# A second batch of attention in float32 products, and subtractions moved from GpSimd to VectorE

## The chip, the cores and the metric

The kernel runs on one core of one Trainium2 chip. The metric is device time in microseconds (us), the median of several runs of one execution each. A core has TensorE (matrix products, written PE, its weight loads PEld), VectorE (DVE), ScalarE (ACT), GpSimd (POOL) and SyncE (SP, here the queue that issues all transfers).

## The reference, cut to what matters

Eight batches of 576 tokens with 512 features go through three blocks, all in float32:

```
q, k, v: (8, 8, 576, 64); attention inside chunks of 64 tokens
  scores = q k^T / 8;  p = softmax(scores);  x = p v          -> (8, 576, 512)
token and channel mixer, for each batch
  u  = x + (relu(x^T w_tok1) w_tok2)^T       w_tok1 576x256, w_tok2 256x576
  x2 = u + relu(u w_ch1) w_ch2               w_ch1 512x1536, w_ch2 1536x512
gated mixer
  h  = relu(x2 w_in);  u, v = the halves of h (512 each)
  v  = (v - mean) / sqrt(var + 1e-6)
  v  = w_spatial v + b_spatial               along the 576 tokens
  out = (u * v) w_out
```

## The kernel before, in words

A float32 factor is split into a half-precision high part and a half-precision low part (`hi = f16(x)`, `lo = f16(x - hi)`), and a product is three half-precision products (hi hi, hi lo, lo hi) that add up in PSUM. The high part is made by ScalarE, the low part by a subtraction on VectorE or GpSimd.

**Weights.** The weights come as 64-bit floats. 24 chunks (list `W`) of up to 1024 columns: 0 and 1 are w_tok1, 2 and 3 w_tok2, 4 to 9 w_ch1, 10 to 15 w_ch2, 16 to 19 w_in, 20 and 21 w_out, 22 and 23 w_spatial (float32, 1440 columns). `w_steps` (lines 115 to 157) gives a chunk's four steps: `upper` (L127, L129) and `lower` (L133) build the float32 from the two words on VectorE, `high` (L140 scales in place, L141 makes the high part; L143 alone for the first six chunks) is ScalarE's, `low` (L148) is GpSimd's, except for the first six chunks, whose subtraction is done by TensorE (L153, L154) and brought back by ScalarE. Loads go to three stage buffers in turn (six for the first six chunks), the float32 to two temporaries in turn. `w_tick` moves the list on by one step, with two chunks under way; `w_until(i)` ticks until chunk i is done.

**Attention.** A group is 128 tokens of a batch (five groups, the last of 64). Batch 0 (`first_steps`, lines 406 to 473) uses float32 products on 64x64 quarters of TensorE: 32 score products a group, maximum and subtraction on VectorE out of PSUM (L426, L427), the exponential on ScalarE, the normalisation on VectorE (L436 to L439), four transposes on TensorE (L444), copied back by ScalarE, and 64 products with v, which give the output both ways round (L455, L457), with the low part by VectorE (L470). Batches 1 to 7 (`at_steps`, lines 230 to 394) have 20 steps a group: load, split q and k (`qk_hi`, `qk_lo`), score products in half precision, softmax (L303 to L314), split p (L317 and, on GpSimd, L320), transpose p by a transfer (L321), split v (L327, L331), products with p, split the output (L383 and, on GpSimd, L386) and transpose it by a transfer (L387). Batch 1 (`ACC`) adds up its three products in PSUM; batches 2 to 7 put the parts side by side in one product (`stack`, `cross_s`, `add_s`, `cross_x`, `add_x`).

**Order.** From line 735 on TensorE's order is as written; the other engines' orders are planned when the program is built, with the written order as priority. Products run through `products`, which calls `pump` after each one: a clock of TensorE's time at full speed, which starts attention steps of the next batch (`attention_from`, spread over 80 us for batch 1 and 118 us after) and weight ticks (one in 1.7 us during batch 0's channel products, one in 3 us from the gate on). PSUM has four tiles of two banks, shared by all.

A batch is: `tok1` (L534, L538), `tok2` (with a residual, L548 to L550), `ch1` (12 blocks of 24 products, L511), `ch2` (4 blocks of 72 products), `gate_v` (statistics L628 to L638, on GpSimd the power L636 and the low part L645), the next batch's `tok1`, then `gated` (`gate_u` and `spatial`), the next `tok2` and the output product L689. In batch 0, `ch1(m)` waits in the written order for chunk 4 + m // 2 and `ch2` for chunk 15; `ch1` of batch 0 is evicted twice by ScalarE (L586, L587) with its low part on GpSimd (L588), in the other batches by L590 and, on VectorE, L591. The residual of `ch2` has its low part on GpSimd for blocks 0 to 2 and on VectorE for block 3 (L557).

Of the kernel before, what the change touches and what calls it, by code (L numbers as in the profile page):

```python
# [15 lines left out]
ACC = 1  # L16
# [10 lines left out]
def mixer_kernel(ctx: ExitStack, tc, qk0, qk, v, wt1, wt2, wc1, wc2, win, wsp, bsp, wout, out):  # L27
# [87 lines left out]
    def w_steps(i):  # L115
# [92 lines left out]
    def at_load_qk(g):  # L208
        b, i, n = geo(g)
        own, cross, cs = ranges(n)  # L210
        if b == ACC:
            SP.dma_start(
                out=qk32.rearrange("p h c t -> p (h c t)")[:, 0:8 * n],
                in_=qk0[b, :, i * 1024:i * 1024 + 8 * n],
            )
            return
# [13 lines left out]
    def at_steps(g):  # L230
# [4 lines left out]
        m = {"acc": b == ACC}  # L235
        xT = xTs[b % 2]

        flat = qt.rearrange("p h s t -> p (h s t)")
        parts = [flat[:, e * 1024:e * 1024 + 8 * n] for e in range(2)]
        raw = qk32.rearrange("p h c t -> p (h c t)")[:, 0:8 * n]  # L240

        def qk_hi():
            if m["acc"]:
                ACT.activation(out=parts[0], in_=raw, func=AF.Copy)
                return
            ACT.activation(out=qt[:, :, own], in_=qk32[:, :, cs], func=AF.Copy)
# [8 lines left out]
        def stack():  # L255
            if m["acc"]:
                return
# [5 lines left out]
        def score():  # L263
            m["sp"] = sp = pm.tile([128, 2, 512], F32, tag="m", name="mp").rearrange(
                "p a (h c t) -> p (a h) c t", h=4, c=2)
            if m["acc"]:
                m["sc"] = sp[:, :, 0, :]
                hi, lo = [p.rearrange("p (s h t) -> p s h t", s=2, h=4) for p in parts]
                for c in range(nc_):
                    t = slice(c * 64, c * 64 + 64)  # L270
                    for h in range(H):
                        r, hh = (LOW, HIGH)[h // 4], h % 4
                        for e, (x, y) in enumerate(((hi, hi), (hi, lo), (lo, hi))):
                            PE.matmul(out=sp[64 * c:64 * c + 64, h, 0, :], lhsT=x[r, 0, hh, t], rhs=y[r, 1, hh, t],
                                      start=(e == 0), stop=(e == 2))
                return
# [5 lines left out]
        def cross_s():  # L282
            if m["acc"]:
                return
# [5 lines left out]
        def add_s():  # L290
            if m["acc"]:
                return
            sd = m["sc"] = m["sd"]
# [4 lines left out]
        def shift():  # L298
            if m["acc"]:
                m["sd"] = sdp.tile([128, H, 64], F32, name="sd")  # L300
            sd, sc = m["sd"], m["sc"]
            m["mx"] = mx = sm.tile([128, H, 1], F32, name="mx")
            DVE.tensor_reduce(out=mx[rows], in_=sc[rows], axis=AX.X, op=ALU.max)  # L303
            DVE.tensor_tensor(out=sd[rows], in0=sc[rows], in1=mx[rows].to_broadcast([n, H, 64]), op=ALU.subtract)  # L304
# [29 lines left out]
        def attend():  # L334
            m["av"] = av = pm.tile([128, 2, 512], F32, tag="m", name="mp").rearrange(
                "p a (k e t) -> p (a k) e t", k=2, e=2)
            if m["acc"]:
                for h in range(H):
                    e = h % 2
                    for c in range(nc_):  # L340
                        q = slice(c * 64, c * 64 + 64)
                        for f in range(2):
                            PE.matmul(out=av[64 * e:64 * e + 64, h // 2, 0, q], lhsT=v16[:, c, h // 2, 2 * e + f, :],
# [507 lines left out]
```

## Time and profile before

| | us |
|---|---|
| median of 3 runs (lowest, highest) | 1207.16 (1206.79, 1207.28) |
| the profiled execution, its own time | 1207.75 |
| its span, first to last instruction | 1206.0 |

| engine | busy us | share of the span | instructions |
|---|---|---|---|
| TensorE products | 1139.4 | 94% | 9472 |
| TensorE weight loads | 820.1 | 68% | 9472 |
| VectorE | 746.8 | 62% | 1256 |
| ScalarE | 458.2 | 38% | 698 |
| GpSimd | 286.9 | 24% | 229 |

The profile is one execution. Times in it are from the span's start. A row of the timeline gives start, duration, engine, line, operation, what it writes and reads, and in brackets the engine's idle time before it and what ended that. "PEclk" and "granted clock" are the share of TensorE's full clock that it had. Batch 0's `tok1` starts at 46.05 us, its first gate product at 179.8 us, and the `tok2` of batch 1 at 244.4 us.

### The profile page before, as it was taken

How to read it: one execution, taken by the hardware profiler on the slowest of the kernel's cores; microseconds unless marked ns; L12 is line 12 of the kernel's file. 1: busy time of each engine (PE TensorE's matmuls, PEld its weight loads, DVE VectorE, ACT ScalarE, POOL GpSimd, SP SyncE). 2: the span in 40 equal slices, each digit the busy share in tenths (PEclk: the TensorE clock that was granted, in tenths of full speed). 3: DMA queues.
4: the chain of work that ended last, by engine and by line, in shares of the span. 5: the costliest groups of instructions: out<-in, count | busy, mean ns of one | idle time of the engine just before them, and what ended most of it. 6: DMA issues, size and time to landing. Idle time of an engine off the chain costs nothing. (4 is left out here: it accounts for less than half of the span.)

```text
span 1206.0 us, 22087 instructions
## 1 busy us (share of the span) xinstructions
PE 1139.4 (94%) x9472; PEld 820.1 (68%) x9472; DVE 746.8 (62%) x1256; ACT 458.2 (38%) x698; POOL 286.9 (24%) x229
## 2 busy tenths in 40 slices
PE   6786887799999999999999999999999999999998
PEld 5464663578757786678857786678858786677765
DVE  6899978865667655865557654775567532542141
ACT  4556444444244433344334433443333422221021
POOL 0167734311122112310222111320232011300120
PEclk9898889799999999999999999999999999999999
DMA  9646444232312412132212422232212211000001
GB/s 334 198 150 187 121 123 129 44 71 66 75 29 60 97 49 67 44 71 50 75 35 57 105 55 66 45 71 45 66 49 45 62 27 36 1 1 1 10 27 44
DMA packets 97138, 87.08 MB, mean 72 GB/s; under 512 B 75664, under 2 KB 76816, under 8 KB 94736
## 3 DMA queue, kind: packets, MB, share of 16 engines
q1 hardware_dynamic: 97040, 85.68, 26.6%
q8 instruction: 74, 1.21, 0.4%
q14 instruction: 24, 0.20, 0.1%
HBM read 59.70 MB, written 9.44 MB: 57 GB/s over the span
## 5 line engine op out<-in xcount | busy, mean ns | idle before, releaser
L511 PE MATMUL mp<-hb,c2w 128*128 128x288 f16 x2304 | 292.7, 289 | 5.4 <-DVE sd L304 3.7
L511 PE MATMUL mp<-xb,c1w 128*128 128x288 f16 x2304 | 289.8, 287 | 5.5 <-DVE sd L304 1.7
L511 PEld LDWEIGHTS <-c1w 128*128 128x128 f16 x2304 | 224.9, 98 | 65.1 <-issue 6.6
L511 PEld LDWEIGHTS <-c2w 128*128 128x128 f16 x2304 | 225.4, 99 | 64.2 <-DVE sd L304 4.0
L591 DVE SCALAR_TENSOR_TENSOR hb<-mp,hb 128x576 f16<-128x576 f32 x84 | 63.2, 753 | 103.5 <-ACT hb L590 103.3
L511 PE MATMUL mp<-spw,vn 128*128 128x288 f16 x896 | 118.8, 290 | 6.5 <-DVE vt L625 4.1
L386 POOL TENSOR_TENSOR xh<-xT,xh 128x512 f16<-128x512 f32 x28 | 38.1, 1362 | 295.5 <-ACT xh L383 251.0
L511 PEld LDWEIGHTS <-vn 128*128 128x128 f16 x896 | 87.6, 99 | 30.3 <-issue 4.3
L511 PE MATMUL mp<-xb,inw 128*128 128x288 f16 x768 | 99.3, 286 | 0.0
L689 PE MATMUL mp<-otw,gb 128*128 128x512 f16 x432 | 96.0, 379 | 0.0
L590 ACT ACTIVATE hb<-mp 128x576 f16<-128x576 f32 x84 | 54.3, 646 | 104.2 <-PE mp L511 104.0
L511 PE MATMUL mp<-inw,xb 128*128 128x512 f16 x384 | 86.0, 384 | 4.8 <-ACT xb L556 4.7
L511 PEld LDWEIGHTS <-inw 128*128 128x128 f16 x768 | 75.1, 98 | 20.5
L320 POOL TENSOR_TENSOR p<-sd,p 128x512 f16<-128x512 f32 (+1 forms) x35 | 42.3, 1210 | 138.7 <-ACT p L317 129.1
L689 PEld LDWEIGHTS <-gb 128*128 128x128 f16 x432 | 42.1, 98 | 47.9
L331 DVE SCALAR_TENSOR_TENSOR v<-v,v 128x512 f16<-128x512 f32 (+1 forms) x70 | 47.5, 705 | 42.8 <-ACT v L327 42.4
L511 PEld LDWEIGHTS <-xb 128*128 128x128 f16 x384 | 37.7, 99 | 51.6 <-ACT xb L556 5.2
L557 POOL TENSOR_TENSOR xb<-rt,xb 128x576 f16<-128x576 f32 x24 | 34.0, 1418 | 159.6 <-ACT xb L556 159.6
L555 DVE SCALAR_TENSOR_TENSOR rt<-mp,xT 128x576 f32<-128x576 f32 x32 | 24.2, 757 | 69.3 <-PE mp L511 68.8
L327 ACT ACTIVATE v<-v 128x1024 f16<-128x1024 f32 (+1 forms) x35 | 33.9, 969 | 62.4 <-PE mp L350 62.4
L511 PE MATMUL mp<-t2w,hb 128*128 128x288 f16 x384 | 52.8, 292 | 3.7 <-ACT hb L540 3.0
L628 DVE BATCH_NORM_STATS2 st<-vt 128x6 f32<-128x512 f32 (+1 forms) x40 | 27.6, 691 | 45.2 <-ACT vt L622 44.9
(152 smaller groups left out, 1475.6 us busy)
## 6 DMA issues: line engine op xcount, KB each, us to landing
qk<-in_qk SPq DMA_DIRECT2D x28, 512.0 KB, 3.8
v<-in_v SPq DMA_DIRECT2D x56, 256.0 KB, 3.8
out<-o SPq DMA_DIRECT2D x31, 256.0 KB, 2.0
vn<-in_wc SPq DMA_DIRECT2D x4, 1024.0 KB, 5.9
otw<-in_wc SPq DMA_DIRECT2D x3, 1024.0 KB, 5.2
spw<-in_wc SPq DMA_DIRECT2D x3, 1024.0 KB, 4.7
hb<-in_qk SPq DMA_DIRECT2D x4, 512.0 KB, 8.0
otw<-in_win SPq DMA_DIRECT2D x2, 1024.0 KB, 6.0
```

What stands on the lines that cost most here:

```text
L320: POOL.tensor_tensor(out=p16[rows, :, 1], in0=m["sd"][rows], in1=p16[rows, :, 0], op=ALU.subtract)
L327: ACT.activation(out=hi_lo[:, :, OWN], in_=v_in, func=AF.Copy, scale=SX)
L331: DVE.scalar_tensor_tensor(out=hi_lo[:, :, 1 + e], in0=v_in[:, :, e], scalar=SX, in1=hi_lo[:, :, 3 * e], op0=ALU.mult, op1=ALU.subtract)
L386: POOL.tensor_tensor(out=m["lo"], in0=xT[:, :, tk], in1=m["hi"], op=ALU.subtract)
L511: PE.matmul(out=o, lhsT=l, rhs=r, start=(i == 0), stop=(i == len(seq) - 1))
L555: DVE.scalar_tensor_tensor(out=t, in0=ps, scalar=DN10, in1=two(x[:, m]), op0=ALU.mult, op1=ALU.add)
L557: eng.tensor_tensor(out=xl, in0=t, in1=xh, op=ALU.subtract)
L590: ACT.activation(out=hh, in_=ps, func=AF.Relu)
L591: DVE.scalar_tensor_tensor(out=hlo, in0=ps, scalar=0.0, in1=hh, op0=ALU.max, op1=ALU.subtract)
L628: DVE.bn_stats(out=st[0:n], in_=t[0:n])
L689: PE.matmul(out=ps, lhsT=gb[:, l, k, tk], rhs=otw[:, r, k], start=(k == 0 and e == 0), stop=(k == 3 and e == 2))
```

## The change

Three things are done. Batch 1 takes the float32 attention of batch 0 (`first_steps` becomes `wide_steps`, with the buffers of the later batches for q, k and v), so the branches for it in `at_steps` go. The low part of every weight chunk from 6 on is one VectorE instruction (`s * scale - hi`), so ScalarE's scaling in place goes, and batch 0's `ch1` is evicted as in the other batches; batch 0's `ch2` has all its low parts on VectorE. And batch 0's `ch2` runs two blocks at a time with k outside, each two k waiting in the written order for their own chunk, from chunk 10. In the beginning, the five q, k loads (and those of v) all go ahead of the first weight load, and weight ticks start at tick 9, not 6.

```diff
         def high():
-            if i >= BY_PE:
-                ACT.activation(out=s, in_=s, func=AF.Copy, scale=scale)
-                ACT.activation(out=hi, in_=s, func=AF.Copy)
-            else:
-                ACT.activation(out=hi, in_=s, func=AF.Copy, scale=scale)
+            ACT.activation(out=hi, in_=s, func=AF.Copy, scale=scale)
...
             if i >= BY_PE:
-                POOL.tensor_tensor(out=lo, in0=s, in1=hi, op=ALU.subtract)
+                DVE.scalar_tensor_tensor(out=lo, in0=s, scalar=scale, in1=hi, op0=ALU.mult, op1=ALU.subtract)
                 return
...
+    def wide_qk(g):
+        b, i, n = geo(g)
+        to = first_qk[:, i * 1024:i * 1024 + 8 * n] if b == 0 else one_qk[:, 0:8 * n]
+        SP.dma_start(out=to, in_=qk0[b, :, i * 1024:i * 1024 + 8 * n])
+
+    def wide_v(b, c0, to):
+        c1 = c0 + to.shape[1]
+        for r, half in enumerate((LOW, HIGH)):
+            SP.dma_start(out=to[half].rearrange("p c h d -> p c (h d)"),
+                         in_=v[b, 64 * c0:64 * c1, r * 256:r * 256 + 256].rearrange("(c k) f -> k c f", k=64))
...
+        steps = [[f] for f in (score, shift, expo, norm, turn, turned, attend, out_hi, out_lo)]
+        if b == 0:
+            return steps
+        steps = [[lambda: wide_qk(g)], [], [], []] + steps
+        steps[5].append(lambda: wide_v(b, 2 * i, vals))
+        return steps + [[]] * (NA - len(steps))
...
-            live[g] = at_steps(g)
+            live[g] = wide_steps(g) if g < 2 * NT else at_steps(g)
...
-    def ch1(m, relax=False):
+    def ch1(m):
...
-        if relax:
-            t = wrk.tile([128, 2, 288], F32, tag="t", name="ht")
-            ACT.activation(out=t, in_=ps, func=AF.Relu)
-            ACT.activation(out=hh, in_=t, func=AF.Copy)
-            POOL.tensor_tensor(out=hlo, in0=t, in1=hh, op=ALU.subtract)
-            return
...
+    def ch2(ms, x):
+        pss = [psum2() for _ in ms]
+        for k in range(12):
+            for i, m in enumerate(ms):
+                mc = slice(m * 128, m * 128 + 128)
+                for e, (a, r) in enumerate(((0, 0), (0, 1), (1, 0))):
+                    for o, s in zip(pss[i][0], HALF):
+                        PE.matmul(out=o, lhsT=c2w[:, a, k, mc], rhs=hb[:, k, r, s], start=(k + e == 0), stop=(k == 11 and e == 2))
+                        pump(288)
+            if len(ms) > 1 and k % 2 and k < 11:
+                w_until(11 + k // 2)
+        for i, m in enumerate(ms):
+            residual(pss[i][1], m, x, DVE if m == 3 or len(ms) > 1 else POOL)
+            DVE.tensor_copy(out=xt[:, m], in_=xb[:, :, m, 512:576])
...
-        first_load(0)
-        first_load(1)
...
+        wide_qk(0)
+        wide_qk(1)
+        wide_v(0, 0, first_v)
         for i in range(2, 5):
-            first_load(i)
+            wide_qk(i)
+        for _ in range(6):
             w_next()
...
-        if tick >= 6:
+        if tick >= 9:
             w_tick()
...
-                ch1(m, b == 0)
-            if b == 0:
-                w_until(15)
-            for m in range(4):
-                ch2(m, x)
+                ch1(m)
+            for ms in ((0, 1), (2, 3)) if b == 0 else ((0,), (1,), (2,), (3,)):
+                if b == 0:
+                    w_until(10)
+                ch2(ms, x)
```

## Rows read from the trace of the kernel before

**Rows 1.** The page: engine shares, and GB/s in 40 slices of the span.

```profile
PE 1139.4 (94%) x9472; PEld 820.1 (68%) x9472; DVE 746.8 (62%) x1256; ACT 458.2 (38%) x698; POOL 286.9 (24%) x229
...
GB/s 334 198 150 187 121 123 129 44 71 66 75 29 60 97 49 67 44 71 50 75 35 57 105 55 66 45 71 45 66 49 45 62 27 36 1 1 1 10 27 44
```

**Rows 2.** Windows: us; busy (count) of PE, PEld, DVE, ACT, POOL; PEclk; DMA share, GB/s.

```profile
64.60:129.40 64.80, 45.68 (x498) 34.69 (x496) 64.66 (x57) 36.86 (x51) 43.52 (x20) 0.91 0.53 160
...
42.50:152.40 109.90, 85.85 (x877) 61.47 (x877) 108.59 (x92) 64.66 (x87) 70.65 (x32) 0.90 0.51 156
```

**Rows 3.** Timeline of VectorE, single instructions.

```profile
42.51 0.69 DVE L127 TENSOR_SCALAR gb<-vn 128x1024 uint32<-128x1024 uint32 x1 [3.30 <-issue]
...
47.08 1.22 DVE L250 TENSOR_TENSOR qt<-qk,qt 128x1024 f16<-128x1024 f32 x1
...
72.26 1.25 DVE L312 TENSOR_SCALAR mx<-mx 128x8 f32<-128x8 f32 x1
...
112.47 0.16 DVE L312 TENSOR_SCALAR mx<-mx 128x8 f32<-128x8 f32 x1
...
113.35 0.69 DVE L314 TENSOR_TENSOR sd<-sd,mx 128x512 f32<-128x512 f32 x1
```

**Rows 4.** Timeline of GpSimd, one instruction.

```profile
71.66 1.82 POOL L588 TENSOR_TENSOR hb<-ht,hb 128x576 f16<-128x576 f32 x1 [7.79 <-ACT hb L587]
```

**Rows 5.** Windows of L127, L129, L133, L314, L312, L331, L250 alone, in this order.

```profile
42.50:152.40 109.90, 14.82 (x14) 0.90 0.51 156
...
42.50:152.40 109.90, 25.32 (x14) 0.90 0.51 156
...
42.50:152.40 109.90, 27.47 (x14) 0.90 0.51 156
...
42.50:152.40 109.90, 8.32 (x4) 0.90 0.51 156
...
42.50:152.40 109.90, 3.89 (x4) 0.90 0.51 156
...
42.50:152.40 109.90, 9.19 (x8) 0.90 0.51 156
...
42.50:152.40 109.90, 6.98 (x5) 0.90 0.51 156
```

**Rows 6.** The page's costliest groups: one of VectorE.

```profile
L591 DVE SCALAR_TENSOR_TENSOR hb<-mp,hb 128x576 f16<-128x576 f32 x84 | 63.2, 753 | 103.5 <-ACT hb L590 103.3
```

**Rows 7.** Timeline of TensorE.

```profile
37.62 0.66 PE L444 MATMUL mp<-gb,sd 64*128 64x64 f32 x4 [3.59 <-DVE sd L439]
...
46.05 5.34 PE L534 MATMUL mp<-x,t1w 128*128 128x512 f16 x24
...
72.79 8.99 PE L511 MATMUL mp<-xb,c1w 128*128 128x288 f16 x72
```

**Rows 8.** TensorE's groups from 25.9 to 28.4 us: busy us, mean ns, idle before.

```profile
L455 PE MATMUL mp<-p,hb 64*64 64x64 f32 x32 | 1.7, 230 | 0.0
...
L419 PE MATMUL mp<-hb 64*64 64x64 f32 x16 | 0.7, 224 | 0.0
```

**Rows 9.** Windows of TensorE's products with w_ch2, behind chunk 19.

```profile
152.40:179.80 27.40, 21.94 (x160) 0.88 0.50 117
```

**Rows 10.** Waits of TensorE, 42 to 260 us: total, times, longest.

```profile
PE mp L350 <- DVE hb L541: 6.2, 1, 6.2
...
PE mp L511 <- ACT xb L556: 4.7, 1, 4.7
PE mp L511 <- DVE vt L625: 4.1, 1, 4.1
PE mp L279 <- DVE qt L261: 4.0, 1, 4.0
```

**Rows 11.** L637 on VectorE: the timeline's first, then the window.

```profile
194.43 0.22 DVE L637 SCALAR_TENSOR_TENSOR e<-y,z 128x1 f32<-128x1 f32 x1 [0.45 <-POOL y L636]
...
179.80:244.40 64.60, 10.22 (x5) 0.87 0.31 88
```

More of the change, by code (lines that the diff above doesn't have):

```diff
@@ L210, in at_load_qk @@
         own, cross, cs = ranges(n)
[L211 to L215, printed above, removed]
-            return
         SP.dma_start(
@@ L265, in score @@
                 "p a (h c t) -> p (a h) c t", h=4, c=2)
[L266 to L276, printed above, removed]
             for h in range(H):
@@ L336, in attend @@
                 "p a (k e t) -> p (a k) e t", k=2, e=2)
[L337 to L343, printed above, removed]
-                                      rhs=pT[:, h, q], start=(f == 0), stop=(f == 1))
-                return
             for h in range(H):
@@ L356, in cross_x @@
         def cross_x():
-            if m["acc"]:
-                ACT.activation(out=xT[:, :, tk], in_=m["av"][:, :, 0, rows], func=AF.Copy)
-                return
             m["xo"] = t = atp.tile([128, 4, 128], F32, name="xo")
@@ L454, in attend @@
                     x0 = h // 2 * 128 + 64 * c
-                    PE.matmul(out=av[e, r, x0:x0 + 64], lhsT=first_v[half[r], 2 * i + c, h], rhs=pt[half[r], h, t],
+                    PE.matmul(out=av[e, r, x0:x0 + 64], lhsT=vals[half[r], c, h], rhs=pt[half[r], h, t],
                               start=True, stop=True)
                     PE.matmul(out=av[t, r, 256 + 64 * h:320 + 64 * h], lhsT=pt[half[r], h, t],
-                              rhs=first_v[half[r], 2 * i + c, h], start=True, stop=True)
+                              rhs=vals[half[r], c, h], start=True, stop=True)
         def out_hi():
@@ L583, in ch1 @@
         hh, hlo = two(hb[:, m, 0]), two(hb[:, m, 1])
-        if relax:
-            t = wrk.tile([128, 2, 288], F32, tag="t", name="ht")
-            ACT.activation(out=t, in_=ps, func=AF.Relu)
-            ACT.activation(out=hh, in_=t, func=AF.Copy)
-            POOL.tensor_tensor(out=hlo, in0=t, in1=hh, op=ALU.subtract)
-            return
         ACT.activation(out=hh, in_=ps, func=AF.Relu)
         DVE.scalar_tensor_tensor(out=hlo, in0=ps, scalar=0.0, in1=hh, op0=ALU.max, op1=ALU.subtract)
-    def ch2(m, x):
-        outs, ps = psum2()
-        mc = slice(m * 128, m * 128 + 128)
-        products(outs, three(lambda k: c2w[:, 0, k, mc], lambda k: c2w[:, 1, k, mc], 12, lambda e, k: hb[:, k, e]))
-        residual(ps, m, x, DVE if m == 3 else POOL)
-        DVE.tensor_copy(out=xt[:, m], in_=xb[:, :, m, 512:576])
+    def ch2(ms, x):
[12 more added lines that the diff above has]
+            DVE.tensor_copy(out=xt[:, m], in_=xb[:, :, m, 512:576])
     def gate_u(m):
@@ L713, in mixer_kernel @@
     with tc.manual_schedule(engines={mybir.EngineType.SP}):
-        first_load(0)
-        first_load(1)
-        for r, half in enumerate((LOW, HIGH)):
-            SP.dma_start(out=first_v[half].rearrange("p c h d -> p c (h d)"),
-                         in_=v[0, :, r * 256:r * 256 + 256].rearrange("(c k) f -> k c f", k=64))
+        wide_qk(0)
+        wide_qk(1)
+        wide_v(0, 0, first_v)
         for i in range(2, 5):
-            first_load(i)
+            wide_qk(i)
+        for _ in range(6):
             w_next()
-        for _ in range(3):
-            w_next()
-    steps = [first_steps(i) for i in range(5)]
+    steps = [wide_steps(i) for i in range(5)]
     for tick in range(3 * 4 + 9):
@@ L727, in mixer_kernel @@
             if 0 <= tick - 3 * i < 9:
-                steps[i][tick - 3 * i]()
-        if tick >= 6:
+                for f in steps[i][tick - 3 * i]:
+                    f()
+        if tick >= 9:
             w_tick()
```

50 lines of the change are left out of this document (17 added, 33 removed).

## The prediction, made before the changed kernel was run

> **What bounds the kernel now.** The page comes first: TensorE is busy for 94% of the span [rows 1], so most of the run is TensorE's, and a change on other engines pays only where TensorE waits. The windows by stage show where that is. From 42.5 to 152.4 us VectorE is busy for 108.6 of 109.9 us, while TensorE has 85.9 us at a granted clock of 0.90 [rows 2]. That is the stretch in which weight chunks 6 to 19 of 24 are split. From there to the first gate product, at 179.8 us, TensorE leads; from 179.8 to 244.4 us (gate, next token product, spatial) it waits again, and behind 244.4 us nothing of the change is executed, so only the shift in time is carried on. Three stretches are costed: the start, 42.5 to 179.8 us, and 179.8 to 244.4 us.
>
> Busy is not work. With GpSimd idle (before 49 us) the first VectorE step of a 1024-column chunk takes 0.69 us, and an instruction with two 1024-column inputs 1.22 us [rows 3]. Once GpSimd has work they grow. L312, eight columns wide, takes 1.25 us at 72.26, while GpSimd runs from 71.66 for 1.82 us, and 0.16 us at 112.47, with GpSimd idle [rows 3, 4]. One engine holds up the other, and that is the time that the change can free.
>
> **Part 1, VectorE from 42.5 to 152.4 us.** *Freed:* what the rows of the stretch have over the free price [rows 3, 5]: L127 14.82 - 14 x 0.69 = 5.2; L129 25.32 - 14 x 1.22 = 8.2; L133 27.47 - 14 x 1.22 = 10.4; L314 8.32 - 4 x 0.69 = 5.6; L312 3.89 - 4 x 0.16 = 3.3. Together 32.7 us. In this stretch the change leaves GpSimd nothing but the first subtraction of batch 2, so I free all of it. *Removed:* batch 1's splitting of v (L331, 9.19) and of q, k (L250, 6.98) [rows 5], 16.2 us. *Added:* 14 low halves of weights, two inputs of 1024 columns, at 1.22 = 17.1; 12 low halves of the first channel product at 0.753, by the same instruction in later batches [rows 6], = 9.0; four low halves of batch 1's output (512 columns; the nearest row is again 0.753) = 3.0. That is 29.1 us. Batch 1's maximum, shift and sums stay what they were. Net: -32.7 - 16.2 + 29.1 = -19.8 us. The new weight instruction lies between 0.753 (a narrower one that reads PSUM) and the 1.22 taken, or over that by what the scaling in it may cost, at most another 0.69, the price of L127's two operations: -6.5 to +9.7 us over 14. I take the row with the same operands.
>
> A rule speaks against all this. The Trainium skill, Perfetto Trace Analysis, Identifying the Most-Contended Engine, has it that occupancy is a fair measure of how near VectorE is to its roofline. By it a VectorE that is 99% occupied has nothing to free, and 29.1 us added make the kernel slower; the trace disagrees, with 0.16 and 1.25 us for one instruction. It is the third rival below.
>
> **Part 2, the start (0 to 46 us).** The same instructions in another order: attention loads of 512 and 256 KB go ahead of the first weight chunk on SP's queue, and splitting starts three ticks later. Bad end: 0.77 MB at the 334 GB/s of the first slice [rows 1] are 2.3 us. Good end: TensorE waits 3.59 us at 37.62 for the last group's normalisation [rows 7] with chunk 4's products queued behind it, and VectorE then idles for 3.30 us before 42.51 [rows 3], as chunk 6 takes chunk 4's buffer. These are one chain. I take 1.5 us gained, as both waits stand in the rows, and VectorE's work before its idle time is the same.
>
> **Part 3, TensorE up to the gate.** A wide group costs at full clock 32 score products (2 x 0.7 us), four transposes (0.66) and 64 attention products (32 in 1.7 us, the other 32 beside them) [rows 7, 8]: 3.5 us with their overlap, 15.8 us for the four and a half groups. From the first token product to where chunk 19 is done TensorE owes: 28 products of 512 columns, 5.34 x 28/24 = 6.2; 48 + 288 + 128 of 288 columns at 8.99/72 = 0.125, 58.0 [rows 7] (160 of the second channel product's 288 come behind 152.4 us [rows 9]); attention 15.8. Sum 80.0 us. It has from 44.5 (46.0 - 1.5) to 152.4 - 1.5 - 19.8 = 131.1 us, that is 86.6 us, and would have to run at 92% of full speed. Before 152.4 us, with VectorE full, it moved 128 products, 16.0 us, in the 23.0 us from 129.4 us: 70%, the attention between them not counted. I take 85%, the middle between that and no loss, since VectorE holds it a fifth less. Then 73.6 us are done and 6.4 us, 51 products, are late. Behind chunk 19 come (160 + 51) x 0.125 = 26.4 us, and 5.4 us for batch 2's attention and waits (of the 27.4 us now, 20.0 are products and 7.4 the rest, with a wait of 4.0 us for stacked keys [rows 10], of which I leave half). The gate starts at 131.1 + 31.8 = 162.9 us instead of 179.8: **16.9 us**. Bounds: at 92% 25.4 us are left, 156.5 us, 23.3 gained; at 70% 60.6 us are done and 19.4 late, 44.8 are left, 175.9 us, 3.9 gained.
>
> The pairs of the second channel product need one weight chunk per two k, so it begins with chunk 10 done and not 15. Against that, a pair holds two of four PSUM tiles for 144 products, 18 us, and both its residuals come at its end, four VectorE instructions of 0.753; the next pair may wait for one eviction, up to 1.5 us. Both lie within the 85%. The last residual's end is what the gate waits for now, 4.7 us [rows 10]; I count no gain there, the cover being that wait itself. SP's queue loses two transposes a group and half of v's bytes; the next group's q, k load waits for TensorE's score instead of for VectorE, with weight loads queued behind it. Three stage buffers cover that: nothing, or once a 1 MB load, 3 us, if one is used up. ScalarE loses 18 scalings and 12 copies, and isn't on the path: nothing.
>
> **Part 4, 179.8 to 244.4 us.** Five L637, 0.22 us when free, take 10.22 us [rows 11], about 9 of them held up by GpSimd's four weight subtractions and its own gate work. TensorE's waits behind them are 6.2 and 4.1 us [rows 10]. The four subtractions become VectorE's: 2 x 1.22 + 2 x 1.72 (1440 columns) = 5.9 us. Bounds: both waits gone, 10.3 gained; or 5.9 lost, if the gate's own four GpSimd subtractions, which stay, hold VectorE as long. I take 4 gained, as the excess of L637 alone is larger than what is added.
>
> **Sum.** 16.9 (with the start's 1.5 in it) + 4 = 20.9 us. The profiled execution took 1207.75 us (span 1206.0), 0.59 over the median of the runs. 1207.75 - 20.9 = 1186.85, less 0.59: **1186 us**.
>
> **Rivals.** *VectorE alone sets the gate* (TensorE keeps 92%): 23.3 + 4 gained, 1180 us. For it: from 64.6 to 129.4 us TensorE is busy for 45.7 of 64.8 us [rows 2]. Against it: 0.125 us is the spacing of a full stream, so 92% leaves no room for a wait. The Trainium skill, same page and section, judges TensorE's headroom by its weight loads, not by matmul time; they are 34.7 us in that window, 54%, and by that rule this rival would be the likeliest.
>
> *TensorE is held in order.* A wide group's transposes stand two steps behind VectorE's normalisation in TensorE's queue, and channel products behind them. In batch 0 such a wait cost 3.59 us [rows 7]; with ten waits (transposes and attention) of 1.5 us TensorE falls back to 70%: 3.9 + 4 gained, 1199 us.
>
> *Slower.* VectorE's long instructions are its own, or are held by something that stays, as transfers into the same buffers. Place: the splitting stretch. Price: 29.1 - 16.2 = 12.9 us there and 5.9 behind the gate: 1207.75 + 18.8 - 0.59 = 1226 us. It decides if less than 12.9 of the 32.7 us goes; the two rows of L312 speak against it. *No effect* lies at that point, if the terms just cancel.
>
> **How the numbers follow.** A measurement of this kernel tells about 0.2%, 2.4 us. The sum has 0.60 (1178 to 1194), TensorE held 0.20, VectorE alone 0.13, slower 0.05, no effect 0.02. The range reaches from VectorE alone with a better part 4, 1173, to the held case, 1200; it leaves out the slower rivals and the edges. Faster 0.92, same 0.03, slower 0.05.
>
> **What would show it.** L127, L129, L133 at 0.69, 1.22, 1.22 us throughout; GpSimd empty until about 150 us; chunk 19 done at about 131 us; the first gate product at about 163; no change of length behind the spatial products. Wrong if VectorE's rows stay long, if TensorE's waits for the wide groups add up to over 15 us, or if the time behind 244 us differs by more than the shift.

## The result, and the profile after

The changed kernel takes 1179.42 us (median of four runs, 1178.89 to 1183.00) against 1207.03 for the kernel before on the same chip: a ratio of 0.978, 95% interval 0.976 to 0.980. That is 27.6 us less, where 1186 us, some 21 less, was forecast; the range held it.

The profiled execution took 1178.89 us, its span 1177.1. Its line numbers differ: L127, L129 and L133 are still a weight chunk's first three VectorE steps, L144 is the new low half, L551 the low half of `ch1`, L400 the normalisation of a wide group, L405 its transposes, L416 and L418 its products with v, L477 the products of `products`, L560 those of `ch2`, L605 what was L637.

The page after: busy time by engine, and GpSimd's 40 slices.

```profile
PE 1132.4 (96%) x9564; PEld 819.1 (70%) x9564; DVE 719.0 (61%) x1279; ACT 424.9 (36%) x658; POOL 197.7 (17%) x186
...
POOL 0000013201220122211131013201222011200020
```

The timeline of GpSimd after, its first instruction behind those of the first 1.7 us.

```profile
153.48 1.16 POOL L281 TENSOR_TENSOR p<-sd,p 128x512 f16<-128x512 f32 x1 [151.79 <-ACT p L278]
```

GpSimd is empty up to 153.48 us, as meant. In the rows of VectorE this is what became of its long instructions: line, tiles and shapes, count, busy us and mean ns, from 42.5 to 132.5 us.

```profile
L551 DVE SCALAR_TENSOR_TENSOR hb<-mp,hb 128x576 f16<-128x576 f32 x12 | 9.0, 753 | 0.0
L144 DVE SCALAR_TENSOR_TENSOR c2w<-gb,c2w 128x1024 f16<-128x1024 f32 x6 | 7.3, 1221 | 0.0
L129 DVE SCALAR_TENSOR_TENSOR gb<-otw,gb 128x1024 uint32<-128x1024 uint32 x5 | 6.1, 1222 | 0.1
L133 DVE SCALAR_TENSOR_TENSOR gb<-vn,gb 128x1024 uint32<-128x1024 uint32 x5 | 6.1, 1220 | 0.0
...
L127 DVE TENSOR_SCALAR gb<-otw 128x1024 uint32<-128x1024 uint32 x5 | 3.4, 688 | 0.0
...
L398 DVE TENSOR_SCALAR mx<-mx 128x8 f32<-128x8 f32 x4 | 0.7, 167 | 0.0
```

L129 and L133 took 25.32 and 27.47 us for 14 each [rows 5]; now each takes 1.22 us, which is the free price. The eight-column instruction is at 0.167 us in the mean, where two of its rows before were 1.25 and 0.16 [rows 3]. The windows show what the stages made of that (columns as in [rows 2]).

```profile
20.00:46.00 26.00, 19.06 (x236) 12.97 (x227) 22.47 (x37) 14.66 (x25) 0.00 (x0) 0.80 0.69 258
...
42.50:132.50 90.00, 78.05 (x886) 57.32 (x885) 89.71 (x115) 39.15 (x54) 0.00 (x0) 0.98 0.49 167
132.50:159.80 27.30, 25.86 (x261) 20.84 (x262) 19.41 (x35) 10.24 (x15) 1.16 (x1) 1.00 0.53 153
159.80:215.60 55.80, 48.24 (x326) 30.25 (x324) 48.33 (x89) 21.25 (x31) 18.39 (x15) 0.94 0.23 65
```

Chunk 19 is done at 132.5 us (its L144 starts at 131.30 and takes 1.21). In the kernel before it was done at 154.69, with GpSimd's low half (second row); VectorE's own last step of it is the first row, and 152.4 us, which the prediction takes for the end of chunk 19, is where VectorE's unbroken work stops.

```profile
146.72 3.03 DVE L133 SCALAR_TENSOR_TENSOR gb<-otw,gb 128x1024 uint32<-128x1024 uint32 x1
...
152.56 2.13 POOL L148 TENSOR_TENSOR inw<-gb,inw 128x1024 f16<-128x1024 f32 x1
```

VectorE is as full as before, 89.7 of 90.0 us, and its last step from the words of chunk 19 ends 20.1 us sooner (129.6 for 149.7). TensorE's granted clock in this stretch is 0.98 instead of 0.90 [rows 2], so of its two levels, 2.4 and 1.2 GHz, the lower one is almost gone; it is busy for 87% of the stretch, where it was 78%. The first gate product comes at 159.8 us, 20.0 earlier, and the `tok2` of batch 1 at 215.6, another 8.8 earlier. Behind that both kernels take the same time, 961.6 us before and 961.5 after.

TensorE's waits after, from 42 to 235 us (total, times, longest).

```profile
PE mp L405 <- DVE sd L400: 11.1, 4, 5.2
PE mp L302 <- DVE hb L507: 4.6, 1, 4.6
PE mp L477 <- ACT xb L522: 2.5, 1, 2.5
```

The first is the wait that the rival "held in order" named: transposes behind a normalisation. The other two are what is left of the waits of the gate stage [rows 10]: 7.1 us, with the one for the statistics (4.1) gone.

### The profile page after: what moved, and what is told of

Read it like the earlier page. It is cut to its first block, busy times and chain, and to the rows that moved or that the text cites. A ratio compares the mean times of both kernels' runs of the same rounds, so it can differ in the third digit from the quotient of the medians.

```text
span 1177.1 us, 22164 instructions
## 1 busy us (share of the span) xinstructions
PE 1132.4 (96%) x9564; PEld 819.1 (70%) x9564; DVE 719.0 (61%) x1279; ACT 424.9 (36%) x658; POOL 197.7 (17%) x186
## 5 line engine op out<-in xcount | busy, mean ns | idle before, releaser
L477 PE MATMUL mp<-xb,c1w 128*128 128x288 f16 x2304 | 288.9, 287 | 0.0
L560 PE MATMUL mp<-hb,c2w 128*128 128x288 f16 x2304 | 287.7, 286 | 0.0
L477 PEld LDWEIGHTS <-c1w 128*128 128x128 f16 x2304 | 224.8, 98 | 58.1
L560 PEld LDWEIGHTS <-c2w 128*128 128x128 f16 x2304 | 223.5, 98 | 55.8
L551 DVE SCALAR_TENSOR_TENSOR hb<-mp,hb 128x576 f16<-128x576 f32 x96 | 72.3, 753 | 103.5 <-ACT hb L550 103.3
L477 PE MATMUL mp<-spw,vn 128*128 128x288 f16 x896 | 117.9, 288 | 2.7 <-DVE xT L317 2.7
L477 PEld LDWEIGHTS <-vn 128*128 128x128 f16 x896 | 87.1, 99 | 26.3 <-PE mp L477 4.1
L550 ACT ACTIVATE hb<-mp 128x576 f16<-128x576 f32 x96 | 62.2, 648 | 108.8 <-PE mp L477 108.5
L477 PE MATMUL mp<-xb,inw 128*128 128x288 f16 x768 | 99.3, 286 | 0.0
L477 PEld LDWEIGHTS <-inw 128*128 128x128 f16 x768 | 75.2, 98 | 20.4
L477 PE MATMUL mp<-inw,xb 128*128 128x512 f16 x384 | 86.0, 383 | 2.6 <-ACT xb L522 2.5
L281 POOL TENSOR_TENSOR p<-sd,p 128x512 f16<-128x512 f32 (+1 forms) x30 | 34.6, 1155 | 282.3 <-ACT p L278 271.1
L333 POOL TENSOR_TENSOR xh<-xT,xh 128x512 f16<-128x512 f32 x24 | 32.1, 1336 | 289.7 <-ACT xh L330 255.4
L477 PEld LDWEIGHTS <-xb 128*128 128x128 f16 x384 | 37.6, 98 | 49.5 <-ACT xb L522 2.9
L292 DVE SCALAR_TENSOR_TENSOR v<-v,v 128x512 f16<-128x512 f32 (+1 forms) x60 | 36.5, 634 | 40.7 <-ACT v L288 40.3
L596 DVE BATCH_NORM_STATS2 st<-vt 128x6 f32<-128x512 f32 (+1 forms) x40 | 27.6, 690 | 45.9 <-ACT vt L590 45.6
L523 POOL TENSOR_TENSOR xb<-rt,xb 128x576 f16<-128x576 f32 x21 | 29.4, 1400 | 153.2 <-ACT xb L522 153.2
L643 ACT ACTIVATE gb<-gt 128x576 f16<-128x576 f32 x32 | 21.8, 682 | 88.0 <-DVE gt L641 87.7
L477 PE MATMUL mp<-t2w,hb 128*128 128x288 f16 x384 | 51.2, 286 | 1.1 <-ACT hb L506 0.4
```

The source lines that it names most:

```text
L281: POOL.tensor_tensor(out=p16[rows, :, 1], in0=m["sd"][rows], in1=p16[rows, :, 0], op=ALU.subtract)
L292: DVE.scalar_tensor_tensor(out=hi_lo[:, :, 1 + e], in0=v_in[:, :, e], scalar=SX, in1=hi_lo[:, :, 3 * e], op0=ALU.mult, op1=ALU.subtract)
L333: POOL.tensor_tensor(out=m["lo"], in0=xT[:, :, tk], in1=m["hi"], op=ALU.subtract)
L477: PE.matmul(out=o, lhsT=l, rhs=r, start=(i == 0), stop=(i == len(seq) - 1))
L523: eng.tensor_tensor(out=xl, in0=t, in1=xh, op=ALU.subtract)
L550: ACT.activation(out=hh, in_=ps, func=AF.Relu)
```

## The experiments

Twelve kernels ran, each the changed kernel with the edit shown. Their places in the profiled executions, in us: where batch 0's `tok1` is through, where the last L133 of chunk 19 ends (its low half is done 2 to 5 us later), the first gate product, and the time from there to batch 1's `tok2`. What follows that took between 961.4 and 961.6 us in every one, so these columns hold all the differences. They are of one execution each, which can lie off its kernel's median: in e11_both_single it is the longest of four, 1174.92 us, with the other three at 1171.2 to 1171.4.

| kernel | median (ratio, 95%) | tok1 ends | chunk 19 | gate | gate to tok2 |
|---|---|---|---|---|---|
| before | 1207.16 | 52.3 | 149.7 | 179.8 | 64.6 |
| changed | 1179.42 (0.976 to 0.980) | 54.0 | 129.6 | 159.8 | 55.8 |
| e1_start | 1175.99 (0.973 to 0.976) | 51.8 | 126.4 | 156.7 | 56.1 |
| e2_wlow_pool | 1194.97 (0.989 to 0.992) | 53.8 | 134.4 | 174.9 | 56.4 |
| e3_att | 1187.49 (0.983 to 0.986) | 53.9 | 140.1 | 168.5 | 56.4 |
| e4_single | 1183.28 (0.978 to 0.982) | 53.8 | 130.4 | 164.9 | 55.5 |
| e5_read | 1212.34 (1.004 to 1.007) | 53.8 | 158.0 | 192.5 | 56.1 |
| e6_set | 1182.58 (0.977 to 0.981) | 53.9 | 132.2 | 162.6 | 58.5 |
| e7_last4_pool | 1184.56 (0.980 to 0.983) | 53.9 | 130.5 | 162.4 | 59.4 |
| e8_gap | 1174.73 (0.972 to 0.975) | 54.0 | 130.3 | 156.8 | 54.2 |
| e9_gap | 1175.91 (0.973 to 0.976) | 51.9 | 129.5 | 155.9 | 54.7 |
| e10_both | 1177.74 (0.975 to 0.977) | 51.3 | 125.8 | 157.9 | 55.7 |
| e11_both_single | 1171.28 (0.970 to 0.973) | 51.5 | 127.3 | 156.7 | 54.9 |
| e12_early | 1176.51 (0.973 to 0.976) | 52.1 | 127.8 | 162.7 | 50.2 |

### Does GpSimd's work hold VectorE? e5_read, e6_set

Both put some 40 instructions back on GpSimd for which nobody waits: two behind each weight low half up to chunk 19, one behind each `ch1` block of batch 0. In e5_read they read two buffers (first line), in e6_set they only write (the other two; the one-column ScalarE copy sets their pace).

```diff
+    def load_pool(like):
+        POOL.tensor_tensor(out=junk, in0=bB, in1=like, op=ALU.subtract)
...
+        ACT.activation(out=junk[:, 0:1], in_=like[:, 0:1], func=AF.Copy)
+        POOL.memset(junk, 0.0)
...
                 DVE.scalar_tensor_tensor(out=lo, in0=s, scalar=scale, in1=hi, op0=ALU.mult, op1=ALU.subtract)
+                if i < LATE:
+                    load_pool(hi[:, 0:576])
+                    load_pool(hi[:, 448:1024])
```

> The changed kernel with 40 subtractions more on GpSimd that nobody waits for: two for each of chunks 6 to 19 and one for each block of batch 0's first channel product, 576 columns, one input a constant and one the new high part, into a tile that is never read. No data of another engine depends on them. Some 40 x 1.27 = 51 us of GpSimd work. Theory (GpSimd that reads SBUF holds VectorE's two-input instructions): L127, L129, L133, L144 grow as in the kernel before, VectorE needs some 20 to 26 us more to chunk 19, the run takes 1195 to 1206. Rival (the long instructions of the kernel before came from shared data and buffers, not from GpSimd running): rows as in the changed kernel, 1179 to 1181.

> The same places as the run before it, but GpSimd fills a tile (memset, 896 float32 columns, read by nobody) instead of subtracting; a ScalarE copy of one column paces it. The Trainium skill, SBUF - State Buffer, Who interferes with whom, has it that VectorE with two SBUF inputs contends with a GpSimd instruction that reads SBUF, not with one that only writes it. By it L129, L133, L144 stay at 1.22 us, only L127 may grow, the run 1179 to 1184. Rival (any GpSimd work holds VectorE): all four grow, and the run grows with GpSimd's busy time, by about half of it.

Measured: 1212.34 us with the reads, 33 more than the changed kernel and more than was expected; 1182.58 with the writes, as the rule on reads and writes had it. Groups of e5_read from 46 to 158 us (here L149 is the low half, L132 the first step, L395 a maximum out of PSUM, L406 the eight columns, L78 the added subtraction):

```profile
L149 DVE SCALAR_TENSOR_TENSOR c2w<-gb,c2w 128x1024 f16<-128x1024 f32 x6 | 10.8, 1793 | 0.0
...
L132 DVE TENSOR_SCALAR gb<-vn 128x1024 uint32<-128x1024 uint32 x4 | 5.4, 1340 | 0.0
...
L395 DVE TENSOR_REDUCE mx<-mp 128x8 f32<-128x512 f32 x4 | 2.7, 683 | 0.0
...
L406 DVE TENSOR_SCALAR mx<-mx 128x8 f32<-128x8 f32 x4 | 1.5, 364 | 0.0
...
L78 POOL TENSOR_TENSOR junk<-bB,c2w 128x576 f16<-128x576 f32 x12 | 22.4, 1868 | 0.9
```

Groups of e6_set from 46 to 132.2 us (L150 the low half, L133 the first step, L407 the eight columns, L79 the added write):

```profile
L150 DVE SCALAR_TENSOR_TENSOR c2w<-gb,c2w 128x1024 f16<-128x1024 f32 x6 | 7.3, 1212 | 0.0
...
L133 DVE TENSOR_SCALAR gb<-spw 128x1024 uint32<-128x1024 uint32 x4 | 3.7, 929 | 0.0
...
L407 DVE TENSOR_SCALAR mx<-mx 128x8 f32<-128x8 f32 x4 | 1.8, 457 | 0.0
...
L79 POOL MEMSET junk<- 128x896 f32 x38 | 33.6, 883 | 96.4 <-ACT junk L78 96.4
```

The windows from 46 us to the last L133 of chunk 19, first of the changed kernel, then of e5_read, then of e6_set:

```profile
46.00:129.60 83.60, 73.81 (x864) 54.89 (x863) 83.38 (x108) 36.13 (x51) 0.00 (x0) 0.98 0.52 179
```
```profile
46.00:158.00 112.00, 81.90 (x882) 58.95 (x879) 109.92 (x107) 35.83 (x51) 71.80 (x38) 0.91 0.39 133
```
```profile
46.00:132.20 86.20, 75.69 (x857) 55.72 (x856) 85.05 (x107) 42.59 (x89) 33.56 (x38) 0.94 0.51 173
```

The same list of VectorE, 107 or 108 instructions, is 83.4 us of busy time beside an empty GpSimd and 109.9 beside one that reads for 71.8 us: 26.5 us more, 0.37 for each us of GpSimd. Beside one that writes for 33.6 us it is 1.7 us more, 0.05 for each. (The two loads have the same count, 38, and not the same length.) In the rows shown the two-input instruction grows beside reads (1.22 to 1.79 us) and not beside writes (1.21); the one-input first step (L132, L133 in e6_set) and the eight columns grow beside both; the maximum that reads PSUM grows beside neither (0.68). The Trainium skill, SBUF — State Buffer, Who interferes with whom, says just this: a two-input VectorE instruction contends with GpSimd's reads but not with its writes, and `tensor_scalar` can contend with GpSimd in the modes that use both ports. All of these rows agree with it. This is the mechanism on which the forecast rests, with only work added that no other engine waits for. The stage behind the gate is 2.7 us longer in e6_set, though the last write ends at 135.6 us. Its cause isn't shown; the load of chunk 20 lands later there, and its first step starts at 159.46 us, 5.0 later than in the changed kernel.

### What the parts are worth: e3_att, e2_wlow_pool, e7_last4_pool

e3_att gives batch 1 its old attention (half-precision parts, split by ScalarE and VectorE, p's low part on GpSimd); its old branches come back with it.

```diff
-            live[g] = wide_steps(g) if g < 2 * NT else at_steps(g)
+            live[g] = at_steps(g)
```

e2_wlow_pool (chunks 6 to 19) and e7_last4_pool (chunks 20 to 23, `i >= LATE`) put low halves back on GpSimd, with ScalarE's scaling in place.

```diff
         def high():
+            if BY_PE <= i < LATE:
+                ACT.activation(out=s, in_=s, func=AF.Copy, scale=scale)
+                ACT.activation(out=hi, in_=s, func=AF.Copy)
+            else:
                 ACT.activation(out=hi, in_=s, func=AF.Copy, scale=scale)
...
         def low():
+            if BY_PE <= i < LATE:
+                POOL.tensor_tensor(out=lo, in0=s, in1=hi, op=ALU.subtract)
+                return
```

> The changed kernel with batch 1's attention of the kernel before (half-precision parts, ten subtractions on GpSimd, ten transposes by transfers). Theory (the float32 products pay on VectorE): VectorE gets 8 x 0.69 + 4 x 1.22 + 0.69 - 3.0 = 8.1 us more of its own and some 5 us of waiting for GpSimd, TensorE about 4 us less; gate 6 to 13 us later, the run 1185 to 1192. Rival (the float32 products cost TensorE what they save VectorE): the run within 3 us of 1179.4.

> The changed kernel with the low parts of chunks 6 to 19 back on GpSimd (and ScalarE's scaling in place). Theory (GpSimd holds VectorE up, and pays about as much as it takes over): VectorE loses 14 x 1.22 = 17.1 us of work, GpSimd has some 35 us and VectorE's two-input instructions grow by half of that, 17 us; the chain of a chunk gets longer; the run takes 1179 to 1186. Rival (VectorE's busy time is its own work): L127, L129, L133 stay at 0.69, 1.22, 1.22 us and the run gets shorter by up to 15 us, 1165 to 1172.

> The changed kernel with the low parts of chunks 20 to 23 alone back on GpSimd. Behind the first gate product the changed kernel takes 55.9 us to the next second token product, the kernel before 64.6. Theory (GpSimd's four long subtractions held the statistics): 5 to 9 us longer, 1184 to 1188. Rival (the gain there comes from work that was done earlier): within 2 us of 1179.4.

e3_att: 1187.49 us, 8.1 more than the changed kernel, all of it before the gate (168.5). VectorE is full there again, its list longer.

```profile
42.50:140.10 97.60, 82.15 (x814) 58.95 (x812) 97.24 (x118) 45.29 (x59) 14.18 (x7) 0.93 0.60 179
```

The time is within what its theory had. e2_wlow_pool: 1194.97 us, 15.5 more, which neither theory had: both were misses. Fourteen VectorE instructions of 1.22 us, 17.1 us in all, are taken away, and chunk 19 comes 4.8 us *later*. Its window to there, groups of VectorE, and TensorE's wait for the normalisation (here L407):

```profile
42.50:134.40 91.90, 67.88 (x710) 47.48 (x709) 82.38 (x93) 46.88 (x60) 32.88 (x13) 0.91 0.47 156
```
```profile
L133 DVE SCALAR_TENSOR_TENSOR gb<-vn,gb 128x1024 uint32<-128x1024 uint32 x5 | 9.2, 1834 | 0.0
L129 DVE SCALAR_TENSOR_TENSOR gb<-spw,gb 128x1024 uint32<-128x1024 uint32 x4 | 8.6, 2140 | 0.1
...
L127 DVE TENSOR_SCALAR gb<-spw 128x1024 uint32<-128x1024 uint32 x4 | 2.8, 694 | 8.1 <-POOL c1w L148 4.1 <-POOL c2w L148 4.0
```
```profile
PE mp L412 <- DVE sd L407: 13.7, 4, 7.2
```

Two things take the place of the work removed. L129 and L133 are held, up to a mean of 2.14 us. And VectorE is no longer full, 82.4 of 91.9 us: it waits 8.1 us for GpSimd to release one of the two float32 temporaries, since a chunk's buffer is free only when its low half is done. So the subtraction on GpSimd costs twice, once by holding VectorE and once as a longer chain through two buffers. The second was in no theory. Only 4.8 of the 15.1 us by which the gate comes later are there at the last step of chunk 19. The rest is TensorE's: by then it had 710 products out, where the changed kernel had 868 (42.5 to 129.6 us), and behind it works without a break, 40.5 us to the gate instead of 30.2.

e7_last4_pool: 1184.56 us, within what was expected. But of its 5.1 us only 3.6 lie in the stage where the four subtractions run (59.4 us against 55.8). There the instruction that was L637 is held again, and one L133 takes 3.82 us:

```profile
L612 DVE SCALAR_TENSOR_TENSOR e<-y,z 128x1 f32<-128x1 f32 x4 | 6.4, 1605 | 2.2 <-POOL y L611 2.1
L133 DVE SCALAR_TENSOR_TENSOR gb<-hb,gb 128x1024 uint32<-128x1024 uint32 x1 | 3.8, 3823 | 0.0
```

The rest is before the gate (162.4 us for 159.8), where GpSimd has nothing of it to do yet. Of these 2.6 us, TensorE's last wait for the normalisation ends 1.0 later (1.97 us long, to 134.90), and 1.7 are its clock: the 36 products behind that wait take 6.26 us where the changed kernel took 4.58. The windows of that stretch, first of the changed kernel, then of e7_last4_pool:

```profile
135.00:150.00 15.00, 15.00 (x161) 12.01 (x160) 9.14 (x18) 5.93 (x9) 0.00 (x0) 1.00 0.21 46
```
```profile
135.00:150.00 15.00, 15.00 (x147) 11.43 (x147) 7.58 (x14) 5.69 (x9) 0.00 (x0) 0.89 0.16 43
```

So not all of the 5.1 us is GpSimd's.

### The start: e1_start

Loads and splitting begin as in the kernel before: two weight loads ahead of the attention's last ones, ticks from 6 on.

```diff
-        for _ in range(6):
+            w_next()
+        for _ in range(3):
             w_next()
...
-        if tick >= 9:
+        if tick >= 6:
             w_tick()
```

> The changed kernel with the start of the kernel before: loads of q, k and of weight chunks in turn, weight ticks from tick 9 back to tick 6. In the changed kernel chunk 5's last products end at 48.2 us, in the kernel before at 46.05. Theory (the new start lost about 2 us, and all that follows shifts with it): TensorE's first token product runs without a break from about 46 us, the first gate product comes at about 158 instead of 159.8, the run takes 1176.5 to 1178. Rival (VectorE has the same sum of work before chunk 19, and TensorE's position is made up behind it): chunk 19 at the same time, the run within 1 us of 1179.4.

1175.99 us, 3.4 less. Chunk 19 comes 3.2 us earlier and the gate 3.1: VectorE's gain passes to the gate whole. The window of the last part of the start, in the kernel before, then in e1_start:

```profile
20.00:46.00 26.00, 21.25 (x288) 13.62 (x283) 22.54 (x37) 15.90 (x26) 0.00 (x0) 0.87 0.73 266
```
```profile
20.00:46.00 26.00, 20.47 (x253) 12.68 (x246) 22.74 (x37) 15.12 (x26) 0.00 (x0) 0.87 0.66 255
```

TensorE is busier in both than in the changed kernel (19.06 us, granted clock 0.80). There all splitting is late, as two rows of VectorE's timeline show, the first step of chunk 0 and that of chunk 6; below them stands e1_start's of chunk 6.

```profile
18.06 0.48 DVE L127 TENSOR_SCALAR gb<-vn 128x640 uint32<-128x640 uint32 x1
...
45.36 0.69 DVE L127 TENSOR_SCALAR gb<-vn 128x1024 uint32<-128x1024 uint32 x1
```
```profile
42.38 0.69 DVE L127 TENSOR_SCALAR gb<-vn 128x1024 uint32<-128x1024 uint32 x1 [2.60 <-issue]
```

Before, chunk 0 began at 15.27 us and chunk 6 at 42.51 [rows 3]. So the new start costs 2.8 us at its first splitting step, and they are not made up: the changed kernel has lost VectorE's idle time of 3.30 us ahead of chunk 6 [rows 3], but begins that chunk 2.85 us later.

### TensorE held by the normalisation: e8_gap, e9_gap

An empty step before the transposes and one before the products with v give VectorE's normalisation more of TensorE's time. In e8_gap v is loaded as before; the load is then written ahead of the products, so that they use the next group's v. e9_gap loads v two steps later (the last two lines of the diff are its alone); there only the last group of batch 1 takes another v, batch 2's first. Number and shape of all instructions stay.

```diff
+        steps = steps[:4] + [[]] + steps[4:6] + [[]] + steps[6:]
         steps = [[lambda: wide_qk(g)], [], [], []] + steps
-        steps[5].append(lambda: wide_v(b, 2 * i, vals))
+        steps[7].append(lambda: wide_v(b, 2 * i, vals))
```

> The changed kernel with an empty step ahead of batch 1's transposes and one ahead of its products with v, so that VectorE's normalisation has some 2 us more. In the changed kernel TensorE waits four times, 11.1 us in all, for that normalisation. Theory A (TensorE's waits are the slack of a stretch that VectorE bounds): waits fall, VectorE stays full to chunk 19 at about 131 us, the run within 1.5 us of 1179.4. Theory B (the waits are on the path): 1173 to 1177.

> The changed kernel with an empty step ahead of batch 1's transposes and one ahead of its products with v, and the next group's v loaded two steps later, behind those products. The first form of it left TensorE 2.8 us of waits for the normalisation instead of 11.1, with chunk 19 done at the same 130 us, and took 1174.7. Theory B (the waits were on the path): 1173.5 to 1176. Theory A (slack of a stretch that VectorE bounds): 1178 to 1180.

1174.73 and 1175.91 us. Of the 11.1 us of waits 2.8 and 3.7 are left. In e9_gap:

```profile
PE mp L405 <- DVE sd L400: 3.7, 2, 2.8
PE mp L561 <- DVE hb L552: 3.0, 1, 3.0
```

The second line is new: TensorE is further on and waits, early in `ch2` (L561), for a low half of `ch1` that VectorE has not made yet, 3.0 us in e8_gap too.

In e8_gap the start is the changed kernel's (`tok1` through at 54.0 us in both) and chunk 19 comes 0.7 us later, yet the gate 3.0 us earlier. In e9_gap chunk 19 is where it was (129.5 us) and the gate 3.9 earlier; its profiled execution is the shortest of five, and its `tok1` was through 2.1 us sooner, so e8_gap is the cleaner reading. TensorE's order thus had its own part in the gate's time, 3 to 4 us, and both medians lie in theory B's ranges; the 7 to 8 us of waits removed are worth half of their length, and 3.0 us of waiting stand at the new place.

### Pairs and combinations: e4_single, e10_both, e11_both_single, e12_early

e4_single runs `ch2` of batch 0 block by block again, its low parts still on VectorE. e10_both is e9_gap with e1_start's start; e11_both_single adds e4_single to it; e12_early adds chunks 20 and 21 ahead of the gate, by way of the stage buffers of the chunks before, to e10_both. The last group of batch 1 takes batch 2's v in these three too.

```diff
-            for ms in ((0, 1), (2, 3)) if b == 0 else ((0,), (1,), (2,), (3,)):
-                if b == 0:
-                    w_until(10)
-                ch2(ms, x)
+            if b == 0:
+                w_until(15)
+            for m in range(4):
+                ch2((m,), x, b == 0)
```
```diff
-    KW, LATE, BY_PE = 2, 20, 6
+    KW, LATE, BY_PE = 2, 22, 6
...
-                w_until(19)
+                w_until(21)
```

> The changed kernel with batch 0's second channel product one block at a time again, k inside a block, begun with chunk 15 done; low parts of its residual stay on VectorE. In the changed kernel chunk 15 is done at 108.8 us and the second channel product starts at 117.5, so theory (the pairs pay nothing, the weights are there): 1178 to 1180.5, with a wait of the gate's first products of 2 to 4 us as before. Rival (the pairs let TensorE begin earlier): the second channel product starts 3 us later or more, 1182 to 1185.

> The empty steps and the start of the kernel before together. The start alone gave 3.4 us (chunk 19 done 3.2 us earlier), the empty steps about 4.5 (TensorE further ahead when chunk 19 is done). Theory (one shortens VectorE's side, the other TensorE's, and they add up): 1170.5 to 1172.5. Rival (both shorten the same wait): 1173.5 to 1176.

> The same, with batch 0's second channel product one block at a time. With single blocks alone the run took 1183.3, or 1179.6 in one of four, and its profile had a granted clock of 0.77 from 135 to 150 us, behind a wait for the last normalisation that the changed kernel has as well. Theory (the pairs pay nothing and the 4 us were the clock): within 1.5 us of the run before it. Rival (the pairs are worth 4 us): 3 to 5 us longer.

> The empty steps, the start of the kernel before, and chunks 20 and 21 moved up behind chunk 19, into stage buffers that are free by then, ahead of the gate instead of inside it. VectorE idles 5.6 us behind chunk 19 in the changed kernel, and chunks 20 and 21 take it 2 x 4.3 us inside the gate. Theory (these steps stand between the gate's statistics, and TensorE waits for those): 2 to 5 us less than the second run. Rival (the gate's waits come from its own chain): within 1 us of it.

e4_single: 1183.28 us; three runs at 1183 to 1184 and one at 1179.58, while the changed kernel has three at 1179 and one at 1183.00. `ch2` begins at 118.4 us against 117.5, so the time is that of the rival and its reason, a start 3 us later, is not: chunk 15 is long done. The profiled execution, one of the longer ones, differs from 132 us on, in TensorE's last wait for the normalisation and in the clock behind it. The wait in the changed kernel, then the wait and the window of e4_single:

```profile
133.94 0.43 PE L405 MATMUL mp<-gb,sd 64*128 64x64 f32 x4 [1.96 <-DVE sd L400]
```
```profile
136.24 0.66 PE L405 MATMUL mp<-gb,sd 64*128 64x64 f32 x4 [3.40 <-DVE sd L400]
...
136.00:141.00 5.00, 4.76 (x22) 3.18 (x23) 1.27 (x4) 0.38 (x1) 0.00 (x0) 0.50 0.02 3
```

The five microseconds behind the wait are granted 0.50, all at 1.2 GHz, where the changed kernel has 1.00. Of the 5.1 us by which the gate is later, 0.9 are there when `ch2` begins, 1.4 are the longer wait, and 2.8 come from the lower clock. That does not say what the pairs are worth.

e10_both: 1177.74 us, no better than either of its parts, and above both expectations. Chunk 19 is through at 125.8 us, 3.7 before e9_gap's, but the gate at 157.9 comes 2.0 later. From 105 to 120 us TensorE stands idle for 3.9 us and is granted 0.80:

```profile
105.00:120.00 15.00, 11.06 (x127) 8.29 (x120) 15.00 (x20) 5.74 (x9) 0.00 (x0) 0.80 0.42 149
```

Behind chunk 19 it is then busy for 31.6 of 32.1 us: TensorE is the bound. e11_both_single takes 1171.28 us, 6.5 less than e10_both, the shortest of all. Neither expectation had that (the same time, or 3 to 5 us more): with the waits moved, single blocks are faster, where e4_single had them slower or equal. What the pairs are worth depends on where TensorE's waits fall and stays open. e12_early: the stage behind the gate is 5.5 us shorter than e10_both's and the gate 4.8 later; what the gate no longer does is done ahead of it, and the run is 1.2 us shorter, less than the theory's 2 to 5 and more than the rival's 1.

Of the kernels that compute everything, e1_start is the fastest: 1175.99 us, 3.4 below the changed one.

## Why the prediction was right, and where it was not

**Part 1, VectorE: right, and 3 us too small.** It forecast 19.8 us less between chunk 6 and chunk 19. From the first step of chunk 6 the kernel before took 109.9 us to 152.4, the end that the forecast used, and the changed one 87.1 (45.36 to 132.5): 22.8 less. The long instructions are at the free prices, the new low half at the 1.22 us taken, scaling included. The durations of VectorE's instructions add up to 114.5 us in 92 before and to 96.0 in 112 after, 18.5 less, and 2.2 of the 96.0 are work that came behind 152.4 us before. What the sum of durations left out is their overlap: a row's duration is longer than the step to the next. VectorE's timeline after:

```profile
129.50 0.67 DVE L397 TENSOR_REDUCE mx<-sd 64x8 f32<-64x512 f32 x1
130.09 1.21 DVE L232 TENSOR_TENSOR qt<-qk,qt 128x1024 f16<-128x1024 f32 x1
131.23 0.16 DVE L398 TENSOR_SCALAR mx<-mx 64x8 f32<-64x8 f32 x1
```

The 0.67 us row takes 0.59 of the engine's time and the 1.21 one 1.14, 0.07 to 0.08 less. Over all rows the overlap is 9.0 us after and 5.9 before; that gives 3.1 us, and VectorE idles 0.2 us instead of 1.2. The rule that occupancy is a fair measure (the Trainium skill, Perfetto Trace Analysis, Identifying the Most-Contended Engine) does not hold here: e5_read has VectorE busy for 109.9 of 112.0 us with a list that takes 83.4 us alone.

**Part 2, the start: wrong sign.** 1.5 us gained were taken; chunk 6 begins 2.85 us later, and by e1_start the new order costs 3.4 in the end. Even the bad end of the bounds, 2.3 us for the 0.77 MB loaded first, was too good. The step that failed is the choice between the ends: the waits were read as one chain of which the new order would take a part, but TensorE waits for the normalisation as long as before (8.0 us up to 50 us, against 8.1), and all splitting begins later. Whether the loads or the later ticks do that is open, since e1_start puts back both.

**Part 3, the gate: 159.8 us for 162.9.** Chunk 19 came 1.4 us late (132.5 for 131.1): the start lost 4.4 against the forecast, VectorE's stretch won 3.0. By then 96 of the 288 products of `ch2` were out instead of 77: 19 x 0.125 = 2.4 us to the good. And the last stage has 27.3 us, 24.0 of them for the 192 products left, 3.3 for the rest, where 5.4 were taken: 2.1 more. The factor of 85% for TensorE held: by the forecast's prices 74.9 us of work were done in the 86.0 us from 46.5 on, 87% (6.2 for `tok1`, 54.0 for 432 products, 14.0 for four wide groups and 0.7 for the scores of the half one, whose transposes come at 133.94). What was too high is the wide group. A whole group's scores, its transposes and its products with v after, from the timeline and from the groups of 72.5 to 76 us:

```profile
57.51 0.69 PE L380 MATMUL mp<-qk 64*64 64x64 f32 x32
...
116.32 0.63 PE L405 MATMUL mp<-gb,sd 128*128 128x128 f32 x4 [2.17 <-DVE sd L400]
```
```profile
L416 PE MATMUL mp<-pT,v 64*64 64x64 f32 x32 | 1.7, 230 | 0.0
```

That is 3.0 us a group and not 3.5: the 32 score products take 0.69 us, and not twice 0.7. With it the share is 84%.

**Part 4: mis-sized, 4 us taken and 8.8 measured**, inside its bounds. L637 went from 10.22 us [rows 11] to this (L605 alone):

```profile
159.80:215.60 55.80, 2.91 (x5) 0.94 0.23 65
```

TensorE's three waits of this stage were 15.0 us together [rows 10] and are 7.1. The step that failed is the size of what is freed: L637's excess alone was set against the four new subtractions. These cost 5.7 us (two of 1.22, two of 1.65), and with them in it VectorE is busy for 48.33 us of the stage, 6.4 less than in the kernel before:

```profile
179.80:244.40 64.60, 49.55 (x327) 31.10 (x325) 54.72 (x86) 26.30 (x35) 27.10 (x19) 0.87 0.31 88
```

Part of that is three steps of chunk 20, 3.2 us from 154.46 us on, which now run ahead of the gate. And the wait for the last residual, counted at nothing, fell from 4.7 to 2.5 us. e7_last4_pool gives 3.6 us of the stage back; no run isolates the other 5.2. VectorE's steps for the chunks are not free in this stage: e12_early has chunks 20 and 21 ahead of it and takes 5.5 us less there than e10_both.

So of the 28.9 us between the two profiled executions, where 20.9 were forecast, 20.0 lie before the gate (16.9 forecast) and 8.8 behind it (4).

**The rivals.** *Slower* falls: the long instructions were held, by GpSimd's reads. *Held in order*: its waits are there, 11.1 us and below the 15 named, but worth 3 to 4 us by e8_gap and e9_gap, not 13. *VectorE alone* gave 1180 us, nearer to the result than the forecast, yet not by its own steps: its gate would be at 156.5 us, the measured one lies midway between that and 162.9, and what brings the total there is part 4. e1_start (VectorE earlier, the gate as much earlier) and e9_gap (VectorE unchanged, the gate earlier), with e8_gap, show that both engines hold the gate; in e10_both TensorE does.

What each part of the change is worth in the finished kernel: low halves of chunks 6 to 19 15.5 us (e2_wlow_pool), the attention 8.1 (e3_att), the last four low halves 5.1 (e7_last4_pool), the start -3.4 (e1_start). Together 25.3 of 27.6 us; the parts act on each other, as e10_both shows, and the 5.1 have some 1.7 us of TensorE's clock in them, so the rest isn't assigned to the pairs. No run puts back the eviction of `ch1` or the low halves of `ch2`'s residual alone.

## What to carry to other kernels

Where VectorE is full and GpSimd works beside it, compare one instruction's duration with GpSimd idle and with it busy before counting what a moved instruction costs: the difference, times the count, is time that the move frees. Moving work to GpSimd to relieve VectorE can cost twice, since it holds VectorE's two-input instructions and keeps the shared buffers longer. And when one engine's stage gets shorter, the next one's order decides how much of it arrives, so gains of single edits are not added.

## What was not expected of the hardware

GpSimd's writes alone leave VectorE's two-input instructions at 1.21 us, while reads bring them to 1.8. Over a whole stretch a microsecond of GpSimd's reading cost VectorE 0.37 us (e5_read), close to the 0.46 that the kernel before shows (32.7 us freed for 70.65 of GpSimd [rows 2]). And nearly the same TensorE wait was followed by the full 2.4 GHz in the changed kernel (1.96 us; granted clock 1.00 from 135 to 150 us) and by a stretch at 1.2 GHz in e7_last4_pool (1.97 us; 0.89), which made the gate 1.7 us later; what makes the difference no run here tells.
